# First product of a fused convolution and MLP: 48 plain block products in float32r halves in place of 41 float32 Strassen terms, with a new SBUF layout

## The chip, the cores and the metric

One NeuronCore of a Trainium2 chip runs the whole problem. The metric is the device time of one execution in microseconds. The engines are named as the profile names them: PE is TensorE (PEld its weight loads), DVE is VectorE, ACT is ScalarE, POOL is GpSimd, SP is SyncE, which here only issues DMAs.

## The reference

```python
# x: (8, 4096, 192), weight: (8, 7); w = softmax over the 7 taps of each head
x_pad = concatenate([zeros((B, 6, D)), x], axis=1)
out[b, s, h, g] = sum_k w[h, k] * x_pad[b, s + k, h, g]     # a causal depthwise convolution, 24 channels per head
h = out.reshape(32768, 192) @ w_in        # w_in: (192, 2048), the first product
g = h * (1 / (1 + exp(-1.702 * h)))
return g @ w_out                          # w_out: (2048, 192), the second product
```

The weights of the two products arrive in float64 and are rounded to float32 on the chip, in integer and float32 steps on DVE and ACT. The result is float32.

## The kernel before

The 32768 tokens are worked off in 32 big steps; one big step holds two halves of the batch (index n), each with 512 tokens in two parts of 256. For each big step:

- **Convolution.** x is transposed on DVE (`transpose_x`, L518, 32x32 blocks), and the seven taps are multiplied on ACT (`tap`, L570, 128x512) into scratch places in `g`, `osbs` and `room`, then added up by accumulating DMAs on POOL's queue (`add_homes`, L595, 256 KB each) and by adds on POOL (L915). The result is six blocks of 64 channels by 256 tokens in the lower or upper 64 partitions of `conv_t`. A block is also needed in the other 64 partitions; `cross_run` (L609) copies it there with DMAs on SP's queue.
- **First product** (`hidden`). The 64-row blocks are combined by a Strassen-like scheme: 41 terms (`TERMS`), each a sum of blocks of the activation by a sum of blocks of `w_in`. One term is two matmuls (`product1`, L709): the lower 64 partitions into one PSUM bank, the upper 64 into another, 128 columns of weights by 512 tokens, float32. The terms accumulate in four pairs of PSUM banks, and DVE and ACT copy and join partial results between PSUM and SBUF (`copy` L802 and L804, `join` L817) before the GELU on ACT writes `g` (L826 from PSUM, L833 from SBUF). What the engines do, and in which order, is written out by hand in the list `HIDDEN`.
- **Second product** (`second`). Another Strassen-like scheme with 25 products, written out in the list `PLAN`. A "go" is four float32 matmuls side by side (L1207), 128 rows by 32 columns of weights by 256 tokens: three make a main product (`c` = 0 to 2), the fourth is one of the side products. There are 78 of them in a step. The sums of blocks of `g` are made on DVE (`sum`, `add_up` L435 and L437, 128x1024 each) and by accumulating DMAs on POOL's queue (`acc`, L1183, 512 KB). ACT copies side results out (L1232) and seeds PSUM banks (L1236); DVE joins (L435, L437, 96x256), transposes (`turn`, L1126), and SP stores.

All instructions of an engine run in the order in which the program lists them (`manual_schedule`); an instruction that waits holds back whatever stands behind it on that engine. The order is fixed by the lists `HIDDEN` and `PLAN`. The convolution of step s+2 is made during step s and s+1. Pools are not used for double buffering; every place in SBUF is assigned by hand. `("early", i)` in `HIDDEN` starts six of the sums of the second product while the first still runs.

The first big step is different (`first_step`, `second_first`): it rounds the weights piece by piece and does 48 plain float32 products (three blocks of channels by 16 pieces of the output), then a seven-product Strassen scheme for the second product.

Of the kernel before, what the change touches and what calls it, by code (L numbers as in the profile page):

```python
# [8 lines left out]
F32 = mybir.dt.float32  # L9
U32 = mybir.dt.uint32  # L10
# [5 lines left out]
def kernel(  # L16
# [9 lines left out]

# [25 lines left out]
    P = 128  # L52
# [3 lines left out]
    HF = F // 2  # L56
# [8 lines left out]
    UW = HF // NU // 2  # L65
    NJ = T // Q + 1
    XT = NJ * Q
    XW = D - Q
    assert B % 2 == 0 and NC == 3 and D == NC * R and HD == 3 * Q and S % TOK == 0
    assert UW == 2 * P and PAD <= Q and F % (2 * P) == 0  # L70
# [5 lines left out]
    xt_pool = ctx.enter_context(tc.tile_pool(name="xt", bufs=1))  # L76
# [6 lines left out]
    xts = {}  # L83
    xin = consts.tile([P, 2, NJ, XW], F32)
    flat_xin = xin.rearrange("p n j d -> p (n j d)")

    def load_x(big, ns=range(2)):


        p, c = divmod(big, CHUNKS)  # L90
        if c == 0 and 0 in ns:
# [13 lines left out]


    slots = [
        [psum.tile([P, TOK], F32, name=f"slot{i}{h}") for h in range(2)] for i in range(3)
    ]
    sums = [psum.tile([P, TOK], F32, name=f"sums{h}") for h in range(2)]  # L110

    B11, B12, B21, B22 = range(4)
    PAIRS = [(0, 0), (1, 1), (1, 0), (0, 1)]
    NG = 4
    assert len(PAIRS) * 4 == NF == NG * NG
    g = consts.tile([P, NG, 2, 2, NG, T], F32)

    def block(r, j):  # L120

        return g[:, r, j // 2, j % 2, :, :]

    def row(n, i):
        return g[:, i // NG, n, :, i % NG, :]

    room = consts.tile([P, 5, 2 * TOK], F32)
    flat_room = room.rearrange("p i n -> p (i n)")
    osbs = consts.tile([P, 4 * TOK], F32)
    osb = osbs[0 : NC * Q, :].rearrange("q (n j e) -> q n j e", n=2, e=2 * Q)  # L130

    BLK = NG * T
    assert BLK == 2 * TOK
    ROOMS = (1, 2, 3)
    SPOTS = 2 + len(ROOMS)
    KEPT = (4, 0)

    def spot(i):

        if i >= SPOTS:  # L140
            return block(*divmod(i - SPOTS, NG))
        flat = osbs[:, i * BLK : (i + 1) * BLK] if i < 2 else room[:, ROOMS[i - 2], :]
        return flat.rearrange("p (k t) -> p k t", k=NG)

    KS = [
        room[:, 1, :],
        room[:, 3, :],
        room[:, 0, :],
        room[:, 4, :],
        spot(19).rearrange("p k t -> p (k t)"),  # L150
        spot(20).rearrange("p k t -> p (k t)"),
        spot(18).rearrange("p k t -> p (k t)"),
        spot(0).rearrange("p k t -> p (k t)"),
        spot(1).rearrange("p k t -> p (k t)"),
    ]

    KEPT_LATE = 3
    TAP_SPOTS = {0: (10, 16, 15)}
    TAP_HALVES = {1: ((3, 0), (1, 0), (1, 2), (2, 0), (2, 2), (11, 2)), 2: ((13, 0), (13, 2), (11, 0), (16, 2), (13, 0), (11, 0)), 3: ((13, 0), (13, 2), (12, 2), (16, 2), (15, 2), (16, 0))}

    def kept(i):

        if i < NG * len(KEPT):
            return room[0 : NC * Q, KEPT[i // NG], i % NG * T : (i % NG + 1) * T]
        return spot(KEPT_LATE)[0 : NC * Q, i % NG, :]

    NR, FB = 6, None
    NV_B, NV_F, NV_E, NV_S = 6, 1, 2, 1  # L170
    NV_ES = NV_E + NV_S
    OWN_V = 2 * NR
    OWN_ES = OWN_V + NV_B + NV_F
    OVER_ES = OWN_ES + NV_ES
    OVER_F = OVER_ES + NV_ES
    OVER_B = OVER_F + 1 + NV_F
    OVER_C = OVER_B + NV_B
    NB = OVER_C + NR
    conv_t = consts.tile([P, NB, T], F32)
    SPOT_V = {16: (14, 2), 17: (14, 0), 18: (17, 2), 19: (17, 0)}  # L180

    def places_of(big, b):

        if b < NR:
            return b + big % 2 * NR, OVER_F if b == FB and big % 2 else OVER_C + b
        i = b - NR
        if i < NV_B:
            return OWN_V + i, OVER_B + i
        return OWN_V + i, OVER_ES - NV_F + i - NV_B if i >= NV_B + NV_F else OVER_B - 1

    def pair(big, b):

        if b in SPOT_V:
            s, k = SPOT_V[b]
            return spot(s)[:, k : k + 2, :]
        o, x = places_of(big, b)
        return conv_t[:, o : x + 1 : x - o, :]

    def own(big):
        return conv_t[:, big % 2 * NR : big % 2 * NR + NR, :]  # L200

    SUMS_H = [
        (13, 0, "-", 3), (8, 12, "-", 2), (14, 1, "-", 3), (6, 1, "-", 5), (7, 2, "-", 4),
    ]
    SUMS_M = [
        (9, 2, "-", 3), (10, 0, "-", 12), (11, 14, "-", 8),
    ]
    RUNS_C, RUNS_M = [(0, 2)], [(10, 11), (9, 10), (11, 12)]
    SUMS_B_1 = [
        (6, 1, "-", 5), (7, 2, "-", 4), (8, 12, "-", 2), (9, 2, "-", 3), (10, 0, "-", 12), (11, 1, "-", 3),  # L210
        (11, 11, "-", 8),
    ]
    SUMS_F = [(12, 1, "+", 4), (12, 12, "-", 5)]
    SUMS_ES = [
        (13, 0, "-", 3), (14, 1, "-", 3), (15, 1, "-", 11),
    ]
    SUMS_L = [
        (16, 0, "-", 6), (17, 7, "-", 3), (18, 0, "-", 2),
    ]
    SUMS_LH = [  # L220
        (19, 0, "-", 1), (15, 1, "-", 11),
    ]

    NA = 21
    w_in_s = consts.tile([P, NA, UW], F32)
    SUMS_W = [
        [
# [5 lines left out]
        ],  # L235
        [
# [4 lines left out]
        ],  # L241
    ]

    TERMS = [
        [
            (15, 3), (0, 5), (12, 7), (19, 13), (8, 5), (16, 11), (5, 0), (17, 10), (14, 6), (9, 14), (7, 9), (4, 4),
            (3, 19), (2, 4), (1, 14), (10, 18), (18, 16), (13, 8), (11, 17), (20, 18),
        ],
        [
            (12, 12), (19, 3), (7, 15), (3, 10), (5, 11), (17, 1), (2, 4), (15, 7), (10, 9), (0, 6), (6, 2), (9, 0),  # L250
            (16, 8), (13, 10), (18, 2), (11, 11), (14, 6), (1, 3), (8, 1), (4, 9), (20, 0),
        ],
    ]


# [4 lines left out]
    w_form = consts.tile([P, FORMS, NG, HD], F32)  # L260
    WHOLE = 2 * NG

    def form(i):
# [12 lines left out]
        [(23, 1), (24, 1), (1, 14), (7, 0, -1)],  # L276
# [6 lines left out]
    ]  # L283
    TURN_O = (9, 17, 20, 21)


# [3 lines left out]
    PIECE = NC * UW  # L290
    assert PIECE == CW * D and 2 * PIECE <= NR * T and 3 * PIECE <= 2 * NJ * XW and 3 * PIECE <= FORMS * NG * HD
    places = w_in_s[:, 4 * NC : NA, :].rearrange("p a f -> p (a f)")
    b12, b22 = (g[:, r, 1].rearrange("p o i t -> p (o i t)") for r in (1, 3))
    at = [(osbs, 0), (flat_room, 3 * PIECE), (places, 0), (b22, 0)]

    at += at[0:3] + at[0:1]
    assert 5 * PIECE + R <= 10 * TOK and 2 * PIECE <= min((NA - 4 * NC) * UW, 4 * TOK)
    raw = [t[:, i : i + 2 * PIECE].bitcast(U32) for t, i in at]
    diag = b12[:, 0 : 2 * K * R].rearrange("p (c k q) -> p c k q", c=2, k=K)


# [6 lines left out]
    def scratch(flat):  # L308
        return [flat[:, j * PIECE : (j + 1) * PIECE].bitcast(U32) for j in range(2)]
# [1197 lines left out]
```

## Time and profile before

| | |
|---|---|
| median of three runs | 2263.65 us (2262.59 to 2263.84) |
| span of the profiled execution | 2261.7 us |
| busy PE / DVE / ACT / POOL | 99% / 93% / 76% / 44% |
| granted TensorE clock | 0.9 or more of full speed in every slice |
| moved by DMA | 330.45 MB, 146 GB/s |

The profiled execution lies 2 us under the median of the runs. A PE that is busy for 99% of the span is not by itself a proof that PE is the bound, since matmuls overlap; the chain of waits and the spacing of the matmuls tell more.

### The profile page before, as it was taken

The numbers are of one execution on the slowest core, as the hardware profiler recorded it, in microseconds if no ns is written. First come the engines' busy times: TensorE is split into PE (matmuls) and PEld (weight loads), VectorE is DVE, ScalarE is ACT, GpSimd is POOL, SyncE is SP. The second block draws the span as 40 slices with busy tenths as digits, with TensorE's granted clock in tenths as the row PEclk, the third lists the DMA queues.
The fourth block names the chain that finished last, engine by engine and source line by source line (L and its number), as shares of the span: only waits on it lengthen the run. The fifth ranks groups of instructions, "written<-read, shape, count | busy, mean of one in ns | idle before, by whom it ended". The sixth has DMA issues, their size and how long they took to land.

```text
span 2261.7 us, 63910 instructions
## 1 busy us (share of the span) xinstructions
PE 2249.5 (99%) x25090; PEld 1348.2 (60%) x25090; DVE 2112.6 (93%) x3266; ACT 1714.5 (76%) x3342; POOL 989.3 (44%) x1013
## 2 busy tenths in 40 slices
PE   9999999999999999999999999999999999999999
PEld 5455655666656666566665566665666656666655
DVE  8999999999999999999999999999999999999998
ACT  8777787777877777777778777777777877777844
POOL 1544454354543444544445434454344454344510
PEclk9999999999999999999999999999999999999999
DMA  9997768866778767787666886677876768765743
GB/s 205 181 173 144 147 134 162 160 139 138 143 150 169 142 138 146 140 165 152 138 141 136 159 164 141 136 144 147 172 142 138 148 134 165 157 137 113 138 96 71
DMA packets 340988, 330.45 MB, mean 146 GB/s; under 512 B 130161, under 2 KB 279281, under 8 KB 340689
## 3 DMA queue, kind: packets, MB, share of 16 engines
q0 software_dynamic: 66928, 168.65, 42.3%
q1 hardware_dynamic: 272112, 157.32, 30.3%
q8 instruction: 199, 3.26, 0.6%
q14 instruction: 101, 0.82, 0.1%
q10 hardware_dynamic: 1648, 0.39, 0.1%
HBM read 53.15 MB, written 25.17 MB: 35 GB/s over the span
## 4 chain that ended last, share of the span: by engine, by line
PE 96%; DVE 2%; ACT 1%; DMA 1%; issue 0%; POOL 0%; SPq 0%; DVEq 0%; ACTq 0%; POOLq 0%
PE slot L709 37%; PE slot L1207 28%; PE sums L1207 17%; PE sums L709 13%; PE slot L987 1%; DVE g L437 0%; DMA g<-g 0%; PE sums L992 0%; DVE g L817 0%; PE slot L992 0%; DMA xin<-in_x_dram 0%; ACT g L833 0%; DVE xt L518 0%; ACT g L826 0%; DVE room L437 0%
## 5 line engine op out<-in xcount | busy, mean ns | idle before, releaser
L709 PE MATMUL slot<-conv_t,w_in_s 64*128 64x512 f32 x3372 | 826.6, 593 | 1.3 <-ACT slot L802 0.7
L1207 PE MATMUL slot<-g,w_form 128*32 128x256 f32 x5872 | 713.5, 379 | 0.0
L709 PEld LDWEIGHTS slot<-conv_t,w_in_s 64*128 64x128 f32 x3372 | 451.1, 187 | 285.2 <-issue 178.6
L437 DVE TENSOR_TENSOR g<-g 128x1024 f32<-128x1024 f32 x372 | 445.0, 1224 | 9.2 <-ACT g L833 1.9
L1207 PE MATMUL sums<-g,w_form 128*32 128x256 f32 x3800 | 422.0, 379 | 0.0
L1207 PEld LDWEIGHTS slot<-g,w_form 128*32 128x32 f32 x5872 | 365.3, 110 | 89.4
L826 ACT ACTIVATE g<-slot 128x512 f32<-128x512 f32 x494 | 265.1, 625 | 127.9 <-PE slot L709 126.5
L709 PE MATMUL sums<-conv_t,w_in_s 64*128 64x512 f32 x1284 | 350.1, 593 | 0.5 <-ACT osbs L802 0.3
L1207 PE MATMUL slot<-g,w_out_s 128*32 128x256 f32 x4080 | 321.5, 380 | 2.4 <-DVE g L437 1.7
L1183 POOL DMA_DIRECT2D g<-g x124 | 116.4, 939 | 441.7 <-PE slot L1207 302.9
L1232 ACT COPY room<-slot 32x256 f32<-32x256 f32 x434 | 158.5, 365 | 188.7 <-PE slot L1207 174.6
L570 ACT ACTIVATE g<-xt,cw 128x512 f32<-128x512 f32 x389 | 270.3, 719 | 4.8 <-PE slot L992 0.4
L437 POOL TENSOR_TENSOR conv_t<-conv_t 128x256 f32<-128x256 f32 x209 | 195.5, 953 | 156.9 <-PE slot L709 90.6
L1207 PEld LDWEIGHTS sums<-g,w_form 128*32 128x32 f32 x3800 | 211.7, 110 | 69.3
L1207 PEld LDWEIGHTS slot<-g,w_out_s 128*32 128x32 f32 x4080 | 166.1, 110 | 128.5 <-ACT g L826 11.4
L915 POOL TENSOR_TENSOR conv_t<-conv_t,g 128x512 f32<-128x512 f32 x174 | 238.6, 1392 | 4.5
L709 PEld LDWEIGHTS sums<-conv_t,w_in_s 64*128 64x128 f32 x1284 | 171.9, 187 | 106.0 <-issue 58.2
L833 ACT ACTIVATE g<-g 128x1024 f32<-128x1024 f32 x155 | 170.7, 1101 | 0.0
L915 POOL TENSOR_TENSOR g<-g 128x512 f32<-128x512 f32 x87 | 110.7, 1273 | 122.7 <-ACT g L570 120.5
L1232 ACT COPY room<-sums 32x256 f32<-32x256 f32 x217 | 79.3, 366 | 103.6 <-PE sums L1207 91.4
L709 PE MATMUL slot<-g,w_in_s 64*128 64x512 f32 x556 | 150.6, 590 | 0.2 <-DVE slot L817 0.2
L826 ACT ACTIVATE g<-sums 128x512 f32<-128x512 f32 x188 | 103.9, 616 | 58.0 <-PE sums L709 57.5
(254 smaller groups left out, 3912.2 us busy)
## 6 DMA issues: line engine op xcount, KB each, us to landing
g<-g POOLq DMA_DIRECT2D x124, 512.0 KB, 6.5
conv_t<-conv_t SPq DMA_DIRECT2D x844, 64.0 KB, 2.0
xin<-in_x_dram SPq DMA_DIRECT2D x240, 180.0 KB, 6.2
out_dram<-osbs SPq DMA_DIRECT2D x183, 128.0 KB, 2.5
g<-g POOLq DMA_DIRECT2D x65, 256.0 KB, 6.7
g<-g SPq DMA_DIRECT2D x248, 64.0 KB, 3.6
g<-room POOLq DMA_DIRECT2D x31, 512.0 KB, 6.0
g<-osbs POOLq DMA_DIRECT2D x30, 512.0 KB, 6.4
```

Of the source, the lines that this page charges most:

```text
L437: eng.tensor_sub(v(dst), v(a), v(b))
L570: act.mul(home, conv_src(big, c, k), cw[:, c, k : k + 1])
L709: nc.tensor.matmul(slot[h], w_in_s[halves[h], a, v * P : (v + 1) * P], src, start=first, stop=True, skip_group_check=True,)
L826: act.activation(dst[:, :, h, :], ot(bank(src, h)), AF.Gelu_apprx_sigmoid, scale=float(sign))
L833: act.activation(dst.rearrange("p o h t -> p h o t"), src, AF.Gelu_apprx_sigmoid, scale=float(sign))
L915: (vec if eng == "v" else nc.gpsimd).tensor_add(dst, dst, home)
L987: nc.tensor.matmul(chunk(bank, c), w[:, chunk_cols(c)], t, start=first and i == 0, stop=not more and i == len(steps) - 1, skip_group_check ...
L1183: nc.gpsimd.dma_start(out=spot(dst), in_=spot(a), accum_op=ALU.add)
L1207: nc.tensor.matmul(dst, w, t, start=first, stop=last, skip_group_check=True)
L1232: act.copy(to, d)
```

## The change

In the first product the Strassen scheme goes, and with it `TERMS`, `HIDDEN`, the sums of weights and of activations, the joins and the copies. In its place stand 16 items per step (eight column pieces j of 256 hidden units, two halves n), each with three blocks of 64 channels in plain form. Each operand is split into a high and a low half of 12 bits that float32r holds exactly. Per item:

- `upper`: high by high and low by low, 12 matmuls (two operands, three blocks, two halves of the partitions), 128 columns of weights by 512 tokens, float32r, one accumulation;
- `scale`: both banks are multiplied in place by 1 + 2^-12, on ACT or DVE as the list `SCALES` says (one letter per bank; "a" is ACT, "v" is DVE);
- `lower`: the product of the differences, 6 matmuls into the same banks;
- `gelu`: two instructions on ACT.

PE's order is upper(i), lower(i-1), upper(i+1), and so on. The differences of the weights live in DRAM (`wd_dram`) and are read in each step through a ring of three places (`load_ring`). The activation is split at the start of `second` by `high` on ACT and `low` and `both` on DVE, each 128x1536, and each is copied to the other 64 partitions by two DMAs of 384 KB on SP's queue (`cross`). x lands in a quarter of `g`, so the tile `xin` goes. Four of the sums of the second product move from `PLAN` into the last items of the first (`EARLY_G` has ten entries, at items 10 to 15), the other entries of `PLAN` stay but for the "piece" and "late" ones. Step 0's second product is plain, and the convolution of steps 1 and 2 runs on DVE.

The core of the diff, the functions new in it as they stand after:

```diff
-    def product1(slot, a, b, big, v, first=False):
-        both = pair(big, b)
-        for h in range(2):
-            src = both[halves[h], :, :] if h == 0 else both[halves[h], ::-1, :]
-            nc.tensor.matmul(slot[h], w_in_s[halves[h], a, v * P : (v + 1) * P], src, start=first, stop=True,
...
+    C = 2.0**12
+    DOWN, UP = 1.0 - 2.0**-13, 1.0 + 1.0 / C
+    xh, xl, xd = (consts.tile([P, 4 * NC, T], F32R, name=f"x{i}") for i in "hld")
+    def split_high(src, b0, b1):
+        act.mul(xh[:, b0:b1, :], src, DOWN)
+    def split_low(src, b0, b1):
+        vec.tensor_sub(xl[:, b0:b1, :], src, wide(xh[:, b0:b1, :]))
+    def split_both(src, b0, b1):
+        vec.scalar_tensor_tensor(
+            out=xd[:, b0:b1, :], in0=wide(xh[:, b0:b1, :]), scalar=UP, in1=src, op0=ALU.mult, op1=ALU.subtract
+        )
+    def cross(t, to, of, eng=nc.sync):
+        for o in range(2):
+            eng.dma_start(out=wide(t[halves[1 - o], to, :]), in_=wide(t[halves[o], of, :]))
+    def upper(slot, j, n):
+        i, v = piece_of(j)
+        for w, t in ((wh, xh), (wl, xl)):
+            for k in KS:
+                for h in range(2):
+                    nc.tensor.matmul(
+                        slot[h], w[halves[h], i, v, k, :], operand(t, h, 2 * k + n),
+                        start=w is wh and k == KS[0], stop=False, skip_group_check=True,
+                    )
+    def lower(slot, q, n):
+        for k in KS:
+            for h in range(2):
+                nc.tensor.matmul(
+                    slot[h], ring_slot(q)[halves[h], k, :], operand(xd, h, 2 * k + n),
+                    start=False, stop=k == KS[-1], skip_group_check=True,
+                )
+    def scale(slot, engines):
+        for h in range(2):
+            (act.mul if engines[h] == "a" else vec.tensor_scalar_mul)(slot[h], slot[h], UP)
+    def hidden(big, tiles, scales, extra, begun=True):
+        for i in range(NX + 1):
+            if i < NX:
+                if i or not begun:
+                    upper(tiles[i % 4], *divmod(i, 2))
+                scale(tiles[i % 4], scales[i])
+            if i:
+                j, n = divmod(i - 1, 2)
+                q = big * N_W + j
+                lower(tiles[(i - 1) % 4], q, n)
+                gelu(tiles[(i - 1) % 4], j, n)
+                if n == 1:
+                    load_later(q + RING)
+            extra(i)
...
+    SCALES = ["aa", "aa", "va", "vv"] + ["va", "vv"] * 6
...
+        def extra(i, big=big):
+            if i == 0:
+                if big + 2 < N_BIG:
+                    load_x(big + 2)
+                next_tap()
+                add_taps("c2 4", "c2 1", "fin 0", "fin 1")
+            if i == 1:
+                add_taps("c2 3", eng=vec)
+                add_taps("fin 2")
+            if i == 2:
+                next_tap()
+            if i == 3:
+                add_taps("c2 2", "fin 3")
+                next_tap()
+            if i == 4:
+                add_taps("c2 5", "c2 6")
+            if i in (7, 8, 9) and big + 2 < N_BIG:
+                transpose_x(big + 2, i - 7)
+            for j in {10: (0, 3), 11: (4, 1), 12: (5, 2), 13: (6,), 14: (7, 8), 15: (9,)}.get(i, ()):
+                for item in EARLY_G[j]:
+                    sum_g(*item)
...
     PLAN = [
-        ("side", 13, 16, "k0"), ("main", 1, 5, "p2", 1), ("go", 2), ("piece", 1), ("go", 2),
-        ("sum", 14, 14, "-", 18), ("main", 16, 10, "p3", 0), ("go", 2), ("sum", 7, 8, "-", 7), ("go", 2),
+        ("side", 13, 16, "k0"), ("main", 1, 5, "p2", 1), ("go", 1), ("high",), ("go", 3),
+        ("sum", 14, 14, "-", 18), ("low",), ("main", 16, 10, "p3", 0), ("go", 4), ("both",),
...
```

For step 0, `round_w_in` makes the high half of a piece of weights on ACT, the rest on DVE, the low half on ACT and the difference on DVE, 128x384 each, after the rounding that was there before; all 16 items of step 0 scale both banks on ACT. `second_plain` runs 48 rounds of four matmuls of 512 tokens.

More of the change, by code (lines that the diff above doesn't have):

```diff
@@ L180 @@
[L180 to L197, printed above, removed]
@@ L1187, with second @@
     SIDE_HALF = (0, 0, 1, 0, 1, 0, 1)
-    def second(big, bx, by, bs, last):
-        n3 = NC * Q
+    def second(big, bx, bs, by, more, next_first):
         mains, sides = (bs[0], bx[0], by[0]), (bx[1], bs[1], by[1])
@@ L1254, in second @@
             join=lambda d, a, op, b: add_up(value, d, a, op, b), turn=out_turn, store=out_store,
-            tap=next_tap, piece=next_piece, late=late_pieces,
+            tap=next_tap, high=high, low=low, both=both, next=next_first,
         )
@@ L1323, in first_step @@
         transpose_x(0, 0, 0)
-        for k in range(4):
-            conv(0, 0, k, first)
+        for k in range(3):
+            conv(0, k, one)
+        split(in_part(0))
+        high_first(0, 0)
+        high_first(0, 1)
+        for k in range(3, K):
+            conv(0, k, one)
+        high_first(0, 2)
         transpose_x(0, 1, 1)
@@ L1452, in begin @@
-    def begin(big):
-        todo.extend(prepare(big))
-        ready.extend(prepare_taps(big))
-    def fetch(big, slot):
-        v, t = FETCH
-        term(big, v, t, slot, True)
-    def fetch_1():
-        fetch(1, slots[2])
-    first_step(fetch_1)
-    tiles = [slots[2], sums, slots[1], slots[0]]
+        for i in range(NC):
+            split_first(0, i)
+        round_w_in(0)
+        transpose_x(0, 0, 1)
+        conv(0, 0, two, act.mul)
+        high_first(1, 0)
+        high_first(1, 1)
@@ L1473 @@
+        hidden(big, tiles, SCALES, extra)
+        pf, pa, pb, pc = tiles[3], tiles[1], tiles[0], tiles[2]
         if big + 2 < N_BIG:
-            begin(big + 2)
-        second(big, x, y, a, not more)
-        tiles = [f, a, x, y]
+            ready.extend((c, k) for c in (1, 0, 2) for k in range(K))
+        second(big, pb, pa, pc, more, (lambda: upper(pf, 0, 0)) if more else lambda: None)
+        tiles = [pf, pa, pb, pc]
 _INS = ['x', 'weight', 'moe_w_in', 'moe_w_out']
```

1151 lines of the change are left out of this document (333 added, 818 removed), and 66 rows, old and new, of tables (HIDDEN, PLAN, SUMS_O, SUMS_W).

## The prediction

> **What bounds the kernel now.** I read the page first, then the chain of waits in order of time, then one steady big step by windows and by the timeline of PE.
>
> ```profile
> span 2261.7 us, 63910 instructions
> PE 2249.5 (99%) x25090; PEld 1348.2 (60%) x25090; DVE 2112.6 (93%) x3266; ACT 1714.5 (76%) x3342; POOL 989.3 (44%) x1013
> PE 96%; DVE 2%; ACT 1%; DMA 1%; issue 0%; POOL 0%; SPq 0%; DVEq 0%; ACTq 0%; POOLq 0%
> ...
> 1083.63 5.15 PE slot L709 x24
> ...
> 1222.52 5.15 PE slot L709 x24
> ...
> 1007.00:1042.60 35.60, 35.60 (x168) 22.42 (x164) 33.80 (x51) 28.25 (x52) 20.68 (x19) 1.00 0.50 112
> 1042.60:1076.40 33.80, 33.80 (x625) 20.25 (x624) 31.35 (x49) 25.16 (x53) 11.22 (x13) 1.00 1.00 187
> ...
> 1008.01 1.03 PE L709 MATMUL sums<-conv_t,w_in_s 64*128 64x512 f32 x4
> 1008.87 1.03 PE L709 MATMUL slot<-conv_t,w_in_s 64*128 64x512 f32 x4
> ...
> 1005.20 0.39 PE L1207 MATMUL slot<-g,w_out_s 128*32 128x256 f32 x3
> 1005.42 0.39 PE L1207 MATMUL slot<-g,w_out_s 128*32 128x256 f32 x3
> ```
>
> The chain is 96% PE. The same place recurs after 138.89 us for two steps: 69.45 us a step. The windows (columns: PE, PEld, DVE, ACT, POOL, granted clock, DMA share, GB/s) split a step into the first product, 35.6 us, and the second, 33.8 us; PE is busy in all of both. A term of the first product is four records (two halves of the partitions, two weight loads each) and the next begins 0.857 us later: 41 x 0.857 = 35.1 us, and 0.5 us for the change of tile shape. So PE is the bound, with no stall to win. But DVE stands close behind: 33.8 of 35.6 us and 31.4 of 33.8. And in the second product the DMA share is 1.00. A change must not only shorten PE; it must fit into DVE's order and that DMA.
>
> **The price of a float32r matmul.** No row shows one. A float32 pass for 512 columns takes half of 0.857 us, 0.43; for 256 columns the passes are 0.215 us apart. Time goes by columns, and a float32 term is two loaded operands, each streamed once as a record. The new code makes the halves itself, so a pair of matmuls (both halves of the partitions side by side) costs at best a quarter of a term, 0.214 us (one load, a single-width stream), and 0.43 us if the stream stays as it is; 0.857 if nothing is saved. The loads must hide too:
>
> ```profile
> 1010.58 0.19 PEld L709 LDWEIGHTS slot<-conv_t,w_in_s 64*128 64x128 f32 x2 [0.24 <-issue]
> 1011.01 0.19 PEld L709 LDWEIGHTS sums<-conv_t,w_in_s 64*128 64x128 f32 x2 [0.24 <-ACT g L802]
> ```
>
> Both halves load together in 0.19 us while the previous pass runs, just inside 0.214. I take 0.214, since the halving that the doubled records stand for is now done outside. Then 16 items x 9 pairs = 144 pairs x 0.214 = 30.9 us, 4.2 less than 35.1. By the Trainium skill, "FP8 and Floating Point Precision", TensorE Precision Notes, true float32 is four passes and reduced-precision float32 reads 4 bytes and truncates; by it the estimate is 0.857 / 4, the same 30.9 us, and no run here shows it.
>
> **What DVE has to do beside it.** The joins and copies go; what comes is 21 scalings of a bank on DVE and 11 on ACT, and four more sums inside the first product.
>
> ```profile
> 1036.00 1.28 DVE L817 TENSOR_TENSOR sums<-slot,room 128x512 f32<-128x512 f32 x2
> 1037.20 1.21 DVE L437 TENSOR_TENSOR room<-g,osbs 128x1024 f32<-128x1024 f32 x1
> ...
> 1043.19 5.88 DVE L437 TENSOR_TENSOR g<-g 128x1024 f32<-128x1024 f32 x5
> 1048.99 1.22 DVE L437 TENSOR_TENSOR room<-g 128x1024 f32<-128x1024 f32 x1
> ...
> L804 DVE COPY room<-slot 128x512 f32<-128x512 f32 x62 | 40.0, 687 | 9.5 <-PE slot L709 9.5
> L802 ACT ACTIVATE slot<-slot 128x512 f32<-128x512 f32 x32 | 17.3, 581 | 0.0
> ```
>
> Back to back a DVE operation on a PSUM bank takes 0.60 us (two in 1036.00 to 1037.20), a sum 1.16 us (five in 1043.19 to 1048.99). A scaling in place is not in the trace; the PSUM copy (0.687 alone) is nearest, with 0.60 back to back; halved it would be 0.30. I take 0.60.
>
> An item of PE is 9 x 0.214 = 1.93 us. In items 0 to 9 DVE is light. From item 10 on its order is, per item, one or two scalings and then sums: 0.60 + 2 x 1.16 = 2.92; 1.20 + 2.32 = 3.52; 1.76; 2.36; 2.92; and for item 15 1.20 before `lower` can run. That is 14.7 us from the end of `upper`(10), where PE gets to `lower`(15) after 5 x 1.93 + 0.64 = 10.3 us. The scalings stand behind the sums in DVE's order, `lower` behind the scalings, and PE waits 14.9 - 10.3 = **4.6 us** (with 0.2 us for load and signal). At 0.30 for a scaling DVE needs 12.0 us and the wait is near 1.9.
>
> **The taps.** Multiplications of the convolution stand in ACT's order between scalings and GELUs, and the last one (item 3) reuses a place that the sixth add on POOL reads.
>
> ```profile
> L915 POOL TENSOR_TENSOR conv_t<-conv_t,g 128x512 f32<-128x512 f32 x174 | 238.6, 1392 | 4.5
> L915 POOL TENSOR_TENSOR g<-g 128x512 f32<-128x512 f32 x87 | 110.7, 1273 | 122.7 <-ACT g L570 120.5
> L570 ACT ACTIVATE g<-xt,cw 128x512 f32<-128x512 f32 x389 | 270.3, 719 | 4.8 <-PE slot L992 0.4
> ```
>
> POOL starts when the tap of item 0 is done, some 3.3 us into the step (`upper` 1.3, two scalings, the tap); six adds of 1.27 end at 10.9; the tap ends at 11.6, ACT's half of scaling 4 at 12.2, `lower`(4) gets its second bank at 12.4 where PE would take it at 10.3: **2.1 us**, and 2.8 at 1.39 an add. If POOL were early it would be nothing.
>
> **The second product** keeps its 78 goes of 0.431 us and its 0.2 of overhead, 33.8 us. DVE in it: four sums less (-4.6 us), two splittings of 128x1536 more (1.5 x 1.16 each, +3.5). DMA is what changes:
>
> ```profile
> g<-g SPq DMA_DIRECT2D x6, 64.0 KB, 3.5
> conv_t<-conv_t SPq DMA_DIRECT2D x4, 64.0 KB, 4.9
> conv_t<-conv_t SPq DMA_DIRECT2D x2, 128.0 KB, 3.6
> ```
>
> In this window SP copied 0.9 MB between halves beside POOL's accumulations; now it is six DMAs of 384 KB, 2.36 MB. 1.5 MB at the window's 187 GB/s is 8 us more in a stretch at share 1.00. Who waits: accumulations on POOL's queue, read by goes some 10 us later, the copies themselves only at the next step. The price lies between nothing and half of the 8 us, 4 us; I take 0.4, since what is late first is what POOL adds in the next step's item 0. The ring adds 1.57 MB of reads in the first window, whose DMA share is 0.50; SP issues fewer and larger DMAs a step than before and is no bound. `high` stands ahead of ACT's side copies, which have goes to spare.
>
> **A step after:** 30.9 + 0.5 + 4.6 + 2.1 + 33.8 + 0.4 = 72.3 us, 2.9 more than 69.4. Thirty steps: **+87 us**.
>
> **The first steps.**
>
> ```profile
> 21.40:55.70 34.30, 34.30 (x164) 15.18 (x160) 33.92 (x69) 31.54 (x53) 3.60 (x4) 1.00 0.87 201
> 55.70:92.70 37.00, 37.00 (x340) 12.39 (x338) 36.41 (x65) 27.34 (x48) 22.61 (x25) 1.00 0.94 155
> 92.70:136.30 43.60, 42.11 (x173) 23.22 (x172) 41.54 (x82) 38.36 (x72) 17.10 (x20) 1.00 0.99 185
> 136.30:173.20 36.90, 34.47 (x627) 19.83 (x626) 34.76 (x50) 24.76 (x52) 18.02 (x18) 1.00 1.00 191
> ...
> 1036.53 2.06 ACT L826 ACTIVATE g<-slot 128x512 f32<-128x512 f32 x4 [1.49 <-PE slot L709]
> L480 ACT COPY w_form<-w_out_s 128x384 f32<-128x384 f32 x15 | 6.7, 518 | 0.6 <-DMA conv_t<-w_form 0.4 <-DMA w_form<-w_form 0.2
> L553 DVE SCALAR_TENSOR_TENSOR conv_t<-xt,cw,conv_t 128x512 f32<-128x512 f32 x6 | 4.5, 752 | 0.2
> ```
>
> The first product of step 0 took 34.3 us. After, ACT sets it: per piece of weights four operations of 128x384 (0.518) and eight of 512 (four in some 1.95 us), 2.1 + 3.9 = 6.0 us, 6.4 with the turns between ACT and DVE; eight pieces 51 us, and some 12 us until the first halves and their copies are there: 63, +29. The second product is 48 x 2 x 0.43 = 41.2 us and waits some 10 us for the last pieces of `w_out`, rounded behind the GELUs: 51, +14. Step 1's first product has 18 taps ahead of its scalings on DVE, some 12 us: 38.1 + 12 = 50, +7; its second -3. Bounds: 0 if all of this hides, 70 if not. Sum 47; I take **+50**.
>
> **Sum:** 2261.7 + 87 + 50 = 2399 for the profiled execution, and 2 more for the median, which lies 2 us above it: **2400 us**.
>
> **The rivals.**
> - *DVE and ACT keep up (faster).* The sums fall into gaps because a scaling costs half, or the taps are not late: the step is then 30.9 + 0.5 + 33.8 = 65.2, 30 x -4.2 = -127, and 2263 + 50 - 127 = 2186. For it: DVE has some 26 us of work (21 x 0.60, nine sums, three transposes) in 31 us of the first product, so only its order is late. Against: the order is fixed, and the walk through items 10 to 15 leaves out nothing that waits. It decides if the two waits add up to under 2.5 us a step.
> - *Float32r is dearer (much slower).* Here the weights of a pair cannot be loaded while the same half's pass runs: 0.19 + 0.214 = 0.40 us a pair, 144 x 0.40 = 58 us, DVE's waits vanish inside it: 58 + 0.5 + 34.2 = 92.7, +23.3 x 31 + 50, about 3030; with a 0.43 stream about 3150; if float32r saves nothing, far more. Against: the load rows lie inside the passes. The Trainium skill says in "TensorE: Matmul & The Clock Gate", Part 3, The mechanism, that weight loads overlap running matmuls only when the row groups differ; by it this rival holds, and the rows above, a load of either half 0.24 us ahead of its next pass, speak against it.
> - *DMA takes the second product.* The 8 us are half exposed: +3.6 more in 30 steps, 2400 + 108, about 2510.
> - *No change:* the waits add up to just the gain.
>
> **How the numbers follow.** The forecast, 2330 to 2490 with its own bounds (one wait at its lower price, startup 0 to 70, some of the DMA), has 0.58; DMA 0.14; dear float32r 0.09; faster 0.16; about equal 0.03. The range 2200 to 2560 leaves out the dear float32r and the lower half of the faster case. The time is measured to about 0.2%: faster 0.17, within 0.2% 0.02, slower 0.81.
>
> **What would show it.** Right: a pair every 0.214 us inside `upper`; PE idle ahead of `lower` in items 11 to 15, ended by DVE's scalings, about 4 us a step; an idle of 2 us at item 4 ended by ACT; a step of 72 us; steps 0 and 1 some 50 us later than before. Wrong: pairs 0.4 us apart; PE busy through the first product with a step of 65 us; or idle PE in the second product ended by DMA.

## The result, and the profile after

The median after the change is 2510.65 us (four runs, 2507.73 to 2513.16) against 2263.52 us before (four runs, 2262.59 to 2263.84): 1.109 times the time, with a 95% interval of 1.108 to 1.111. The profiled execution spans 2506.8 us, 2 us under its own run's time, as before. The direction and the range of 2200 to 2560 us were right; the forecast of 2400 us took 137 of the 247 us that came, and 2510 lies outside the 2330 to 2490 that it gave as its own bounds.

The page after, its span, its busy times and the shares of its chain of waits:

```profile
span 2506.8 us, 68873 instructions
...
PE 2288.4 (91%) x29078; PEld 1579.1 (63%) x29078; DVE 1813.8 (72%) x2598; ACT 1587.6 (63%) x3131; POOL 715.4 (29%) x719
...
PE 9%; DMA 4%; DVE 2%; POOL 1%; issue 1%; ACT 1%; POOLq 0%; ACTq 0%; DVEq 0%
```

DVE, ACT and POOL are less busy than before, and PE has 218 us without a matmul (2506.8 - 2288.4) where it had 12. The chain's shares, 96% PE before, now add up to less than a fifth of the span: it breaks off early, and the rest of the reading goes by steps. Two records of PE's timeline begin step 2 and step 31, the last:

```profile
245.28 0.97 PE L218 MATMUL slot<-xh,wh 64*128 64x512 f32 x6
...
2428.68 0.96 PE L218 MATMUL slot<-xh,wh 64*128 64x512 f32 x6
```

(2428.68 - 245.28) / 29 = 75.29 us a step, 5.84 more than 69.45. Step 2 begins at 245.3 where it began at 173.2: 72 us later. 72 + 30 x 5.84 = 247 us, the whole difference. The windows (columns as in the prediction) split one steady step, and then steps 0 and 1, into first and second products:

```profile
999.00:1037.70 38.70, 35.14 (x289) 28.66 (x288) 27.70 (x38) 24.11 (x46) 12.25 (x10) 1.00 0.53 116
1037.70:1073.95 36.25, 34.57 (x625) 19.95 (x624) 27.94 (x41) 25.30 (x52) 10.43 (x12) 1.00 0.96 191
24.50:91.40 66.90, 47.72 (x291) 30.26 (x291) 36.55 (x82) 49.48 (x99) 0.00 (x0) 0.83 0.49 139
91.40:144.50 53.10, 45.13 (x385) 20.29 (x384) 30.75 (x58) 18.33 (x33) 13.26 (x15) 0.89 0.64 132
144.50:210.00 65.50, 39.85 (x289) 31.17 (x288) 40.26 (x54) 28.61 (x53) 6.10 (x7) 0.81 0.47 92
210.00:245.20 35.20, 35.20 (x625) 19.34 (x624) 27.94 (x41) 25.26 (x52) 10.42 (x12) 0.96 0.97 196
```

The first product takes 38.7 us where it took 35.6, the second 36.3 where it took 33.8, and PE stands idle in both although DVE is busy for only 28 us of each. The granted clock of PE was 1.00 in the four startup windows before; now it is 0.81 to 0.96 there. PE's timeline in that first product, with what ended each idle time of over half a microsecond:

```profile
1003.94 0.94 PE L227 MATMUL slot<-xd,ring 64*128 64x512 f32 x6
1004.62 0.94 PE L218 MATMUL slot<-xh,wh 64*128 64x512 f32 x6
1005.30 0.94 PE L218 MATMUL slot<-xl,wl 64*128 64x512 f32 x6
...
1011.68 0.96 PE L227 MATMUL slot<-xd,ring 64*128 64x512 f32 x5 [1.23 <-ACT slot L234]
...
1029.28 0.96 PE L227 MATMUL slot<-xd,ring 64*128 64x512 f32 x6 [0.53 <-DVE slot L234]
...
1036.21 1.56 PE L227 MATMUL slot<-xd,ring 64*128 64x512 f32 x6 [1.59 <-DVE slot L234]
```

Three pairs (six records) begin 0.68 us after the three before them: 0.227 us a pair. The waits stand where the prediction put them: item 4, behind ACT's half of a scaling, and the tail, behind DVE's. Over the steady steps the view of waits (who waits for whom, us in total, times, longest) has the same two, and a third place, in the second product:

```profile
PE slot L227 <- DVE slot L234: 61.5, 59, 1.9
PE slot L227 <- ACT slot L234: 35.3, 28, 1.6
PE slot L557 <- DVE g L620: 28.2, 22, 3.2
```

The last is a sum of DVE (line 620) that waits itself. Its cause stands in DVE's timeline and in the list of transfers (KB each, median us from issue to landing):

```profile
1054.89 1.23 DVE L620 TENSOR_TENSOR g<-g,room 128x1024 f32<-128x1024 f32 x1 [1.85 <-DMA g<-g]
...
1059.61 1.23 DVE L620 TENSOR_TENSOR g<-g 128x1024 f32<-128x1024 f32 x1 [1.58 <-DMA g<-room]
```

```profile
g<-g POOLq DMA_DIRECT2D x124, 512.0 KB, 13.6
...
xh<-xh SPq DMA_DIRECT2D x62, 384.0 KB, 3.7
xl<-xl SPq DMA_DIRECT2D x62, 384.0 KB, 6.9
xd<-xd SPq DMA_DIRECT2D x62, 384.0 KB, 12.1
```

In the trace of before the 512 KB accumulations landed in 6.5 us; beside the crossings of the halves they take 13.6. At 1060.89 PE goes on after 1.33 us, for the sum that began at 1059.61.

### The profile page after: what moved, and what is told of

It reads as the page before. It is cut to its first block, busy times and chain, and to the rows that moved or that the text cites. A ratio compares the mean times of both kernels' runs of the same rounds, so it can differ in the third digit from the quotient of the medians.

```text
span 2506.8 us, 68873 instructions
## 1 busy us (share of the span) xinstructions
PE 2288.4 (91%) x29078; PEld 1579.1 (63%) x29078; DVE 1813.8 (72%) x2598; ACT 1587.6 (63%) x3131; POOL 715.4 (29%) x719
## 3 DMA queue, kind: packets, MB, share of 16 engines
q1 hardware_dynamic: 234768, 202.04, 34.2%
## 5 line engine op out<-in xcount | busy, mean ns | idle before, releaser
L239 ACT ACTIVATE g<-slot 128x512 f32<-128x512 f32 x1024 | 551.9, 597 | 275.2 <-PE slot L227 246.7
L227 PE MATMUL slot<-xd,ring 64*128 64x512 f32 x3072 | 561.1, 405 | 136.7 <-DVE slot L234 74.5
L234 DVE TENSOR_SCALAR slot<-slot 128x512 f32<-128x512 f32 x651 | 432.0, 694 | 332.3 <-PE slot L218 328.7
L557 PE MATMUL slot<-g,w_out_s 128*32 128x256 f32 (+1 forms) x6336 | 532.1, 404 | 38.9 <-DVE g L620 29.1
L218 PE MATMUL slot<-xh,wh 64*128 64x512 f32 x3072 | 513.3, 393 | 21.9 <-ACT wh L440 17.1
L227 PEld LDWEIGHTS slot<-xd,ring 64*128 64x128 f32 x3072 | 359.9, 186 | 242.6 <-DVE slot L234 134.9
L218 PE MATMUL slot<-xl,wl 64*128 64x512 f32 x3072 | 507.7, 389 | 4.5 <-DMA xl<-xl 3.4
L218 PEld LDWEIGHTS slot<-xh,wh 64*128 64x128 f32 x3072 | 357.2, 185 | 83.6 <-ACT wh L440 20.8
L218 PEld LDWEIGHTS slot<-xl,wl 64*128 64x128 f32 x3072 | 360.7, 185 | 55.0 <-issue 4.8
L557 PE MATMUL slot<-osbs,w_form 128*32 128x256 f32 x2232 | 226.3, 379 | 0.5 <-issue 0.4
## 6 DMA issues: line engine op xcount, KB each, us to landing
g<-g POOLq DMA_DIRECT2D x124, 512.0 KB, 13.6
```

The source lines that it names most:

```text
L218: nc.tensor.matmul(slot[h], w[halves[h], i, v, k, :], operand(t, h, 2 * k + n), start=w is wh and k == KS[0], stop=False, skip_group_check ...
L227: nc.tensor.matmul(slot[h], ring_slot(q)[halves[h], k, :], operand(xd, h, 2 * k + n), start=False, stop=k == KS[-1], skip_group_check=True,)
L234: (act.mul if engines[h] == "a" else vec.tensor_scalar_mul)(slot[h], slot[h], UP)
L239: act.activation(g[:, r // NG, n, :, r % NG + h, :], slot[h].rearrange("p (o t) -> p o t", o=2), AF.Gelu_apprx_sigmoid,)
L557: nc.tensor.matmul(dst, w, t, start=first, stop=last, skip_group_check=True)
```

## The experiments

Each kernel ran in three rounds or more beside the kernel before on the same chip. "First" and "second" are the products' mean times over steps 2 to 30 (from the first pair of the step to the start of its last one, and from there to the next step), "step 2" the time at which it begins.

| run | median us | ratio to before (95%) | first | second | step 2 |
|---|---|---|---|---|---|
| changed kernel | 2510.65 | 1.108 to 1.111 | 38.6 | 36.7 | 245.3 |
| e1_tail | 2432.29 | 1.071 to 1.076 | 35.8 | 37.2 | 243.7 |
| e2_tap | 2486.15 | 1.097 to 1.100 | 37.8 | 36.7 | 247.2 |
| e3_nocross | 2454.43 | 1.083 to 1.086 | 38.4 | 35.0 | 245.3 |
| e4_keep | 2497.23 | 1.102 to 1.105 | 38.6 | 37.0 | 231.7 |
| e5_acc | 2643.82 | 1.166 to 1.170 | 38.5 | 41.1 | 250.5 |
| e6_three | 2396.05 | 1.057 to 1.060 | 34.9 | 37.1 | 233.1 |
| e7_all | 2305.41 | 1.017 to 1.020 | 33.4 | 35.5 | 232.3 |
| e8_start | 2290.15 | 1.010 to 1.014 | 33.4 | 35.5 | 218.5 |
| e9_noacc | 2352.71 | 1.038 to 1.041 | 34.3 | 36.6 | 218.2 |
| e10_acc1 | 2271.37 | 1.003 to 1.005 | 33.5 | 34.7 | 215.0 |
| e11_last | 2272.51 | 1.003 to 1.006 | 33.6 | 34.7 | 211.7 |
| e12_half | 2284.27 | 1.008 to 1.012 | 34.0 | 34.8 | 213.2 |

**One place at a time.** The tail of the first product:

```diff
-    SCALES = ["aa", "aa", "va", "vv"] + ["va", "vv"] * 6
+    SCALES = ["aa", "aa", "va", "vv"] + ["va", "vv"] * 3 + ["aa", "aa", "va"] * 2
```

> Six of the scalings of the first product's items 10 to 15 go from the vector engine to the scalar engine; nothing else is changed. Theory (the tail of the first product waits for the vector engine's scalings, which stand behind its sums: about 3.2 us of TensorE gaps in each of 30 steps in the trace of the changed kernel): most of these gaps close and the time falls by 50 to 95 us, to 2415 to 2460. Rival (the matrix passes alone set the first product, the gaps are filled otherwise): within 10 us of 2510. Second rival (the scalar engine is late as soon as it has six more evictions): the gaps return behind L234 of the scalar engine and the time is 2510 to 2560.

78 us less, as the theory said. The first product lost 2.8 us a step, the second gained 0.5 and its wait grew: PE's waits for DVE's scalings fell from 62 to 34 us in the view of waits, and those for DVE's sum rose from 28 to 48.

```profile
PE slot L557 <- DVE g L620: 47.5, 27, 4.4
PE slot L227 <- ACT slot L234: 35.1, 28, 1.3
PE slot L227 <- DVE slot L234: 33.5, 29, 2.4
```

The order of GpSimd's tap sums:

```diff
-                add_taps("c2 4", "c2 1", "fin 0", "fin 1")
+                add_taps("c2 4", "c2 1")
...
-                add_taps("fin 2")
+                add_taps("c2 2", "fin 0", "fin 1", "fin 2")
...
-                add_taps("c2 2", "fin 3")
+                add_taps("fin 3")
```

> GpSimd's sums of the taps come in another order: those that item 4's scaling waits for come first, the one of c2 2 goes behind them. Theory (the 1.4 us wait of TensorE near the first product's item 4 is a chain from GpSimd over a tap to the scalar engine's scaling): the wait goes in each of 30 steps, so 30 to 45 us less, 2465 to 2480. Rival (the wait only moves to the next item whose tap now comes later): 2500 to 2515.

24 us less, between the two. The wait for ACT's scaling is gone from the list, so its cause is shown. Some 4 us later in the step waits for the ring's loads are new, 14.7 us in 17 waits or 0.5 us a step:

```profile
PE slot L227 <- DVE slot L234: 61.9, 58, 1.9
PE slot L557 <- DVE g L620: 26.8, 20, 2.7
PE slot L227 <- DMA ring<-wd_dram: 14.7, 17, 2.0
```

The crossings of the low halves and of the differences (four of the six transfers of 384 KB), left out from the steady steps, so that the products read old halves:

```diff
             split_low(own, 0, OVER)
-                cross(xl, OVER_ALL, OWN_ALL)
...
             split_both(own, 0, OVER)
-                cross(xd, OVER_ALL, OWN_ALL)
```

> Leaves out, in each step, the copies of the low halves and of the half differences from one half of the partitions to the other (16 transfers' worth of data of every step that the kernel before did not have); the products then read old halves, so the output is not the reference's. Theory (the second product's waits for its accumulations come from the DMA engines, busy to 0.97 of that stretch): the second product falls from about 36.4 us towards the 34 of before in each of 30 steps, 40 to 75 us less, 2435 to 2470, and the accumulations of 512 KB land in less than 9 us. Rival (the second product is late because the vector engine's sums are late, by its own load): within 10 us of 2510, with the accumulations landing sooner all the same.

56 us less. The second product fell by 1.7 us, no wait for DVE's sum is left in it, and the accumulations land twice as fast:

```profile
g<-g POOLq DMA_DIRECT2D x124, 512.0 KB, 7.2
```

So the crossings cost the second product its waits, by way of accumulations that land late. But 35.0 is not 33.8. The second products of this run are of two kinds; here are one of each, in windows:

```profile
1017.37:1053.19 35.82, 35.82 (x628) 20.87 (x625) 28.35 (x41) 25.42 (x52) 11.32 (x13) 0.95 0.86 162
1091.55:1125.68 34.13, 34.13 (x629) 20.18 (x626) 28.16 (x41) 25.41 (x52) 11.65 (x14) 1.00 0.90 170
```

Of the 29, 14 run at a granted clock of 1.00 throughout and take 34.1 us, 0.3 more than before; the other 15 have a stretch at half clock and take 35.8 in the mean. The 18 second products of the changed kernel that have no such stretch take 36.55. At full clock the crossings therefore cost 36.55 - 34.12 = 2.4 us a step; the last section has more on the clock.

The startup, where step 1's copies of the kept tile stood behind the end of the forms:

```diff
+        add_forms(4)
         return [(m, n, blocks(k)) for (m, n), k in zip(todo + [(1, 1)], keep)]
...
-            if i == n_last:
-                add_forms(4)
-                end_forms()
...
+            if i == 6 and big == 1:
+                end_forms()
```

> Only the startup is changed: in step 1 the scalar engine makes its copies of the kept tile before it turns to the end of the forms, which goes to item 6 of that step. Theory (17 us of TensorE's idle time in step 1 come of that copy standing behind a wait for GpSimd's last form): 10 to 18 us less, 2492 to 2500. Rival (the same time is lost to the next late thing, the vector engine's turn, 18 taps and scalings): 2505 to 2515.

13 us less, and step 2 begins 13.6 us earlier. In the changed kernel's timeline of ACT the cause is plain: negations wait for the last forms (sums of the output weights, made by transfers on GpSimd's queue), and only then the copy of the kept tile (line 574) is made, on which DVE's turn and 18 taps stand:

```profile
150.47 0.52 ACT L308 ACTIVATE w_form<-w_form 128x384 f32<-128x384 f32 x1 [1.92 <-DMA w_form<-w_form]
155.27 0.52 ACT L308 ACTIVATE w_form<-w_form 128x384 f32<-128x384 f32 x1 [4.27 <-DMA w_form<-w_form]
160.24 0.52 ACT L308 ACTIVATE w_form<-w_form 128x384 f32<-128x384 f32 x1 [4.45 <-DMA w_out_s<-w_form]
160.78 0.58 ACT L574 COPY room<-slot 96x512 f32<-96x512 f32 x1
```

**Relief for the transfers that is not one.** The five accumulating transfers become additions on GpSimd:

```diff
-        if op == "acc":
+        if op == "acc" and dst in (14, 15, 7, 12, 18):
+            nc.gpsimd.tensor_add(spot(dst), spot(dst), spot(a))
+        elif op == "acc":
```

> The five accumulating transfers of 512 KB in the second product become additions on GpSimd; the crossings of the halves stay. Theory (the second product waits for accumulations that the full DMA engines land late, 13.6 us instead of 6.5): the wait of the vector engine's sum for an accumulation goes, as with the crossings left out (which gave 56 us): 40 to 65 us less, 2445 to 2470. Rival (GpSimd's additions, 2.6 us each, hold back its other transfers or the vector engine's sums beside them): less than 20 us gained, or a loss, 2490 to 2530.

133 us more: the theory fell, and by more than the rival allowed. The additions take 3.2 us each in the mean, and DVE's own sums of 128x1024, 1.22 us in the changed kernel, took 1.70 in the mean (groups of DVE in the steady steps):

```profile
L620 DVE TENSOR_TENSOR g<-g 128x1024 f32<-128x1024 f32 x345 | 581.3, 1703 | 2.7 <-DMA g<-osbs 1.7
```

What happens shows in the timelines of DVE and POOL of e7, the run after next, which moves two of the five:

```profile
1033.72 0.41 DVE L621 TENSOR_TENSOR room<-slot,room 96x256 f32<-96x256 f32 x1
1034.05 4.21 DVE L621 TENSOR_TENSOR g<-g 128x1024 f32<-128x1024 f32 x2
...
1039.44 2.60 DVE L621 TENSOR_TENSOR room<-room 96x256 f32<-96x256 f32 x1
...
1050.47 0.42 DVE L621 TENSOR_TENSOR room<-room 96x256 f32<-96x256 f32 x1
```

```profile
1032.81 3.23 POOL L626 TENSOR_TENSOR g<-g,room 128x1024 f32<-128x1024 f32 x1 [1.22 <-DVE room L621]
...
1038.35 3.42 POOL L626 TENSOR_TENSOR g<-g 128x1024 f32<-128x1024 f32 x1 [0.59 <-DVE g L621]
```

A sum of 96x256 with both operands in SBUF takes 0.42 us (at 1050.47); the one that begins while GpSimd adds takes 2.60 and ends at 1042.04, 0.27 us after that addition (1041.77). That is a wait for the addition's end rather than a slower sum. The sum at 1033.72 also begins while GpSimd adds (1032.81 to 1036.04) and takes 0.41 us: one of its operands (`slot`) lies in PSUM. The two sums behind it, with all operands in SBUF, are held again, 4.21 us in place of 2 x 1.22. In e5's steady steps it is the same: 30 sums of 96x256 that begin in an addition, with both operands in SBUF, take 2.57 to 2.60 us, and 90 with one in PSUM 0.40 to 0.42. The Trainium skill says in "SBUF — State Buffer", SBUF: two separate sides, that DVE with two SBUF inputs and GpSimd share one pair of ports, and that the one that comes second is blocked for the other's whole instruction. The trace agrees, in the sums that are held and in those with an operand in PSUM that are not; the theory had left it out, and the rival had named it at too small a price. A part of the 133 us may be the clock: this run has 32 stretches of 3.4 us at half clock from step 2 to its end, the changed kernel 12, a difference of at most 20 x 1.7 = 34 us.

**Together.** The three edits e1, e2 and e4 in one kernel:

> Three edits together: the tail's six scalings on the scalar engine, GpSimd's tap sums in the other order, and the scalar engine's copies ahead of the end of the forms in step 1. Alone they gave 78, 24 and 13 us. Theory (three waits at three places, none covers another): the gains add, 115 us less, 2385 to 2405. Rival (what one edit frees is lost at the next late instruction, since the vector and the scalar engine are near full): the sum of gains is under 90 us, 2420 or more.

115 us less, where the sum of the three is 78 + 24 + 13 = 116: independent places. Then a steeper share of the scalings, and two of the accumulations on GpSimd:

```diff
-    SCALES = ["aa", "aa", "va", "vv"] + ["va", "vv"] * 6
+    SCALES = ['va', 'va'] + ['vv'] * 8 + ['aa'] * 6
...
+        if op == "acc" and dst in (15, 12):
+            nc.gpsimd.tensor_add(spot(dst), spot(dst), spot(a))
```

> The three edits of the run before, two of the five accumulations (the last one into 12 and 15) as additions on GpSimd, and a steeper share of scalings: the vector engine takes most of items 0 to 9, the scalar engine all of items 10 to 15. Theory (with the waits of both products gone, a step is set by TensorE's own time and the changed products cost 4 us per step less than the Strassen terms): 2270 to 2320, about the kernel before. Rival (the vector engine, 72 percent busy before, becomes late in items 0 to 9): 2350 to 2400.

2305 us. One step in windows:

```profile
989.90:1023.70 33.80, 33.75 (x301) 27.01 (x295) 26.73 (x37) 25.14 (x48) 12.69 (x10) 1.00 0.56 125
1023.70:1058.75 35.05, 34.49 (x617) 20.19 (x619) 32.02 (x40) 25.79 (x54) 16.45 (x14) 1.00 0.91 180
```

PE is busy through the whole first product, with DVE at 27 of 34 us: the waits of the changed kernel were of order, not of load. But the first product without a wait is 33.4 us, not the 31.4 (30.9 + 0.5) of the prediction. The startup alone was next: half of step 0's scalings to DVE, output weights rounded sooner, step 1's first scalings to ACT.

```diff
-        hidden(0, tiles, ["aa"] * NX, extra, begun=False)
+        hidden(0, tiles, ["va"] * NX, extra, begun=False)
...
-        hidden(big, tiles, SCALES, extra)
+        hidden(big, tiles, ["aa"] * 8 + SCALES[8:] if big == 1 else SCALES, extra)
```

> The run with all edits (2305 us) with three more in the startup alone: in step 0 half of the first product's scalings go to the vector engine and the output weights are rounded two items sooner; in step 1 the scalar engine makes the scalings of items 0 to 7. Theory (step 1's 17.6 us of TensorE idle time come of the vector engine's scalings behind 18 taps of 0.75 us, step 0's 8.5 us of the rounding behind the product, and step 0's pace of the scalar engine's 49.6 busy us in 67): 15 to 30 us less, 2275 to 2290. Rival (the taps themselves or the kept copies are what the first product of step 1 waits for, wherever the scalings run, and the vector engine's rounding work paces step 0): under 8 us gained, 2297 or more.

15 us less, at the near edge of the theory: in step 1 PE's wait before its first `lower` fell from 17.2 us (for DVE, in e7) to 7.2, and ends with ACT now.

```profile
148.64 2.14 PE L227 MATMUL slot<-xd,ring 64*128 64x512 f32 x6 [7.23 <-ACT slot L234]
```

Then the number of accumulations on GpSimd, none and one (`dst in ()`, `dst in (15,)`):

> As the run before in this list, with no accumulation on GpSimd: all five go as accumulating transfers again. Theory (the two moved accumulations relieve the DMA engines, and 5 us of the 90 between the run with three edits and the run with all came of the steeper scalings per step at most): 1.5 to 2.5 us per step are lost again in the second product, 45 to 75 us more than the run before in this list. Rival (the vector engine pays for GpSimd's additions with its own sums, 2.6 us instead of 0.4 for one beside an addition, so that the transfers cost no more): within 15 us of the run before in this list, or faster.

63 us more. The 512 KB accumulations land in 13.9 us again, against 9.6 with two moved. The theory had all of it in the second product; that has 1.1 us a step of it (36.6 against 35.5), and the first product another 1.0 (34.3 against 33.4), where PE waits for the ring's loads, 17.7 us in 17 waits.

> As the first run of this list, with one accumulation on GpSimd (into 15) instead of two. Theory (one taken off the transfers is enough to let the others land in time, and each addition on GpSimd slows the vector engine's sums beside it): 0 to 20 us less than the first run of this list. Rival (the transfers need both taken off): 15 to 40 us more than the first run of this list.

19 us less. One addition on GpSimd is better than none and than two: with none the transfers are late, and each addition holds DVE. The second product is 34.7 us. Last, three small edits (item 13's scalings to DVE, step 0's last three items to ACT, the last forms of step 1 later):

> As the run with one accumulation on GpSimd (2271 us), and three edits: item 13's two scalings go back to the vector engine (the tail of the first product waits 1.9 us for the scalar engine, which has all of items 10 to 15); in step 0 the last three items scale on the scalar engine; in step 1 the scalar engine's last form copies go to item 3 and the end of the forms to item 8. Theory (each step's last TensorE gap is at that tail, and step 1's 6.6 us of idle time stand behind those copies): 0.5 to 0.9 us per step and 5 to 9 us at the startup less, 2236 to 2252, under the kernel before. Rival (the vector engine, with two scalings more among its sums, is late instead): 2262 to 2280, no better than the kernel before.

No gain: 2272.5 against 2271.4. The wait of 1.9 us at the end of the first product, on which the theory stood, is not there: three pairs begin 0.44, 0.49 and 0.34 us after the pair before them, which less the pairs' own 0.227 is some 0.6 us, and the edit left these distances as they were. In step 1 the wait for ACT shrank from 6.2 to 0.3 us, and the next late thing took its place, a load into the ring:

```profile
PE slot L227 <- DMA ring<-wd_dram: 4.8, 1, 4.8
PE slot L227 <- ACT slot L234: 0.3, 1, 0.3
```

No version beat the kernel before. What stands against it in the best ones is the startup, 215.0 - 173.2 = 42 us, and 30 x (69.45 - 68.25) = 36 us is what the steps win back.

**Why a pair takes 0.227 us.** The float32 terms come 0.857 us apart, four times 0.214, and each half of the partitions has a load every 0.43 us; a float32r pair has a load of its own every 0.227. Half of the weights' columns in a third of the passes, which leaves out half of these products:

```diff
-                        slot[h], w[halves[h], i, v, k, :], operand(t, h, 2 * k + n),
+                        slot[h][0 : P // 2] if w is wl else slot[h],
+                        w[halves[h], i, v, k, 0 : P // 2] if w is wl else w[halves[h], i, v, k, :],
+                        operand(t, h, 2 * k + n),
```

> As the run before (2272.5 us), but the passes with the low halves of the weights (a third of the first product's, 48 of 144 pairs a step) load 64 of their 128 columns and write 64 of the 128 partitions of the result, so half of these products is left out. The stream stays 512 columns. Pairs came 0.227 us apart so far, not 0.214 as in the float32 terms (0.857 / 4), and a load takes 0.184 us, one for each pass where float32 had one for every two. Theory (a load and its turn set the distance): these pairs come 0.21 us apart or less, the others 0.227 as before; 48 x 0.013 x 30 = 19 us less, about 2254. Rival (the float32r stream of 512 columns itself takes 0.227 us, whatever is loaded): all pairs 0.227 us apart, 2266 to 2276.

The theory fell. The loads of the changed passes took 0.131 us in place of 0.184, and PE's timeline has them no closer, with the time 12 us longer and not 19 shorter:

```profile
1003.12 0.89 PE L229 MATMUL slot<-xd,ring 64*128 64x512 f32 x6
1003.82 0.89 PE L218 MATMUL slot<-xh,wh 64*128 64x512 f32 x6
1004.51 0.89 PE L218 MATMUL slot<-xl,wl 64*64 64x512 f32 x6
1005.20 2.34 PE L229 MATMUL slot<-xd,ring 64*128 64x512 f32 x12
```

Three pairs now take 0.69 or 0.70 us where they took 0.68 (144 pairs x 0.003 x 30 = 13 us, about the loss), the narrow ones as long as the others. The length of the load does not set the distance at this size. That leaves the float32r stream itself, or something that comes with every load whatever its length; these runs do not separate the two, and that mixing two widths costs 0.003 us a pair isn't explained.

## Why the prediction was right, and where its sizes were off

Against the forecast the first product gave 0.5 us a step more, the second 2.5, and the startup 22 in all: 30 x 0.5 + 30 x 2.5 + 22 = 112, the 111 us between 2400 and 2510.65. The waits that the prediction named as signs of being right came, ahead of `lower` behind DVE's scalings and behind ACT's at item 4; so did one that it named as a sign of being wrong, idle PE in the second product for transfers, by way of DVE's sums.

*The price of a float32r matmul: taken at 0.214 us, 0.227 measured.* The mechanism held: a quarter of a term, loads hidden behind the other pass, and the rival of 0.40 us a pair is dead. But 144 x 0.227 = 32.6 us, not 30.9: 1.7 us a step, 51 us in all. The prediction took the quarter of a float32 term where no row had a float32r pass, and named no value between 0.214 and 0.40. Of the 4.2 us a step that the change was to win, 2.5 were there.

*DVE's order in items 10 to 15, taken at 4.6 us, and the taps, at 2.1.* Both waits are where they were put, and e1 and e2 show their causes. Together they cost 5.2 us (38.6 - 33.4, the latter the first product of e7 that has neither), not 6.7. The taps' one was 1.3 a step (35.3 us in 28 waits). Some of that follows from the slower passes: PE comes to item 15 some 5 x 9 x 0.013 = 0.6 us later, so what it waits for is less late. This error and the one before it all but cancel: 38.1 us were forecast for the first product and 38.6 came.

*The second product, taken at 34.2 us, 36.7 measured.* This is the step that failed: +2.9 against +0.4, 75 us in 30 steps. The bounds were right (nothing to 4 us), the choice near the lower end was not. The argument was that what is late first is needed only in the next step; DVE's rows show a sum in the same product that waits 1.85 and 1.58 us for accumulations. Leaving the crossings out gave 1.7 us of the 2.9 back and 56 us of the time, with more stretches at half clock than before. At full clock the crossings cost 2.4 of the 2.9 (36.55 - 34.12); of the rest 0.15 is the changed kernel's stretches at half clock (36.7 - 36.55), and 0.3 (34.1 - 33.8) stays open.

*The rival "DMA takes the second product"* named the right mechanism and, at 2510, the time that came. That is an accident: it gave the crossings 4.0 us a step, 120 us, and they cost 2.4 us a step at full clock, some 70 us. The rest came from the startup and the first product.

*The startup, taken at +50, 72 measured.* Step 0's first product ran to 91.4 us (+36, forecast +29) with ACT busy for 49.5 of 66.9 us and PE waiting for it at each piece of weights:

```profile
49.92 0.96 PE L218 MATMUL slot<-xh,wh 64*128 64x512 f32 x6 [1.20 <-ACT wh L440]
...
56.57 0.96 PE L218 MATMUL slot<-xh,wh 64*128 64x512 f32 x6 [1.49 <-ACT wh L440]
...
63.22 0.98 PE L218 MATMUL slot<-xh,wh 64*128 64x512 f32 x6 [1.50 <-ACT wh L440]
```

A piece takes 6.65 us (63.22 - 56.57; forecast 6.4). The second product of step 0 is 16 us longer (forecast 14), the first of step 1 22 us (forecast 7). There the sum had the 18 taps ahead of DVE's scalings, but not what stood ahead of the taps: the copy of the kept tile behind ACT's wait for GpSimd's last forms, in the order of ACT. e4 gives it 13 us. With 2 us less in the second product of step 1, the four come to 36 + 16 + 22 - 2 = 72.

*What the forecast's rival of 2186 needed.* e7 shows its condition met: no wait in the first product. It does not bring 65.2 us a step but 68.9: the first product is 2.0 us longer than the 31.4 of the sum (1.7 of it the passes), the second 1.7 longer than 33.8.

## What to carry to other kernels

An average of 72% busy says nothing of an engine whose instructions stand in a fixed order: the edits up to e7 took 205 us away (2510.65 - 2305.41) by moving scalings, sums and copies that were not made fewer. When an operation has no row in the trace, give its price an upper end as well as a quarter that looks natural; 0.013 us on each of 144 x 30 pairs was two fifths of the expected gain. And for a transfer added to a full stretch ask which reader in the same stretch is nearest, not only who reads the data moved: here those were the accumulations beside it.

## What the runs showed of the hardware that I had not expected

*Short waits are paid twice.* In the run without crossings (e3) every second step from 284 to 1605 us has the same 3.4 us at half clock, at the start of the second product, after the tail's waits. Windows of that run:

```profile
1014.00:1018.10 4.10, 2.43 (x19) 1.14 (x19) 4.10 (x6) 1.61 (x4) 0.00 (x0) 1.00 0.11 38
1018.10:1021.50 3.40, 3.40 (x39) 1.74 (x32) 2.27 (x2) 2.30 (x4) 0.00 (x0) 0.50 0.33 87
```

PE was without a matmul for 1.67 of 4.10 us, and then the clock was 0.50 for 3.40 us, 1.7 us lost; that is also the difference of the two kinds of second products above (35.82 and 34.13). Of such stretches the changed kernel has 12 from step 2 to its end, 12 x 1.7 = 20 us at most. Where its second product waits anyway less is lost: the 11 second products with such a stretch take 37.0 us in the mean, the other 18 36.55. The runs without the first product's waits, e7 and later with one or two accumulations on GpSimd, have none between step 2 and the last microseconds. Before step 2 the changed kernel spends 68 us at half clock, the kernel before none; how much of the startup's 72 us that is, no run separates. The Trainium skill, "TensorE: Matmul & The Clock Gate", Part 1, says that the clock falls to a half after an idle window of about 3.4 us, in windows that run free; the length agrees with the trace, the condition does not: here less than half of such a window idle was enough, though not each time.

*GpSimd's additions hold DVE's sums* until they end, 2.60 us in place of 0.42, when both operands of the sum lie in SBUF, and not when one lies in PSUM (0.41).

*A float32r pass of 512 columns takes 0.227 us at full clock,* with one load for each, and no less when the load falls from 0.184 to 0.131 us.
